# A state-space layer gated by a feed-forward layer: two generator sums in one burst, and two shared PSUM banks

## The chip, the cores and the metric

The kernel runs on one core of a Trainium2 chip. The metric is the device time of one execution in microseconds (us), from the first to the last instruction and the little around them. All times below come from timed runs or from one execution that the hardware profiler recorded.

## What is computed

The input `u` has 2048 positions of 512 channels. It is normalised, and then goes two ways whose results are multiplied:

```python
xn = layernorm(u)                               # over the 512 channels
# s: a convolution of each channel with a kernel K of 2048 taps
dt = exp(log_dt);  P[d,n,l] = exp(dt[d] * (A_re + 1j*A_im)[d,n] * l)
K  = einsum("dn,dnl,dn->dl", C, P, dt * B).real # 512 channels, 128 modes each
s  = irfft(rfft(xn, 4096) * rfft(K, 4096))[:2048] + xn * Dskip
# g: a feed-forward layer of width 1792
g  = silu(gelu(xn @ w1 + b1) @ w2 + b2)
out = u + s * g
```

## The kernel before

**Front and back.** The program has a front (the list `ORDER`, up to `gk.close()`) and a back (the convolution by discrete Fourier transforms in matmuls, functions `first_dft` to `rows_out`). In the front two pieces of work are interleaved by hand.

The first is the feed-forward layer. It goes over four blocks of 512 positions and 14 blocks of 128 hidden units, in two passes of 7 hidden blocks; a step j is one pair (positions, hidden block), 56 in all. Each operand is split into a high and a low part, so that each product needs three matmuls of 512 columns. For a step, `F.j.0` and `F.j.1` are the first layer on TensorE (`first_half`, lines 256 to 258, into one of two PSUM banks named f1), `G.j` the gelu on ScalarE (line 270), `H.j` the rounding to the high part on ScalarE (line 276), `R.j` the low part on VectorE (line 282), and `S.j.0` to `S.j.3` the second layer on TensorE (`second_part`, lines 295 to 297, into four PSUM banks named z). `W`, `WB` and `WS` load and split weights: `WS.f.0` and `.1` round the two weight blocks (w1h, w2h) on ScalarE, `.2` and `.3` take the rest (w1l, w2l) on VectorE.

The second is the generator, which makes the convolution kernel K for 16 channels at a time, 32 groups s in all. For each half h of a group, `A.s.h` makes phases by one bf16 matmul (line 595), `B.s.h` rounds them (ScalarE or VectorE), `C.s.h` takes the rest (VectorE, line 609) and so frees the bank. `N.s` takes the sines on ScalarE, `Z.s` the magnitudes on GpSimd, `E.s.0` to `.2` multiply both into tables e on VectorE (lines 641 to 648; two buffers of tables). `Q.s` sums over the 128 modes in 64 small matmul passes (line 656), `U.s` copies the sums out of PSUM on ScalarE (line 662) and `UD.s` stores them by a DMA of the sync engine's queue (SP).

**What sets the order.** Each engine works off its own queue in order. `ORDER` is a list of such pieces: the program emits each piece's instructions in the order of the list, so the list sets every queue's order. Weight DMAs, stores of the sums and reloads all go through SP's queue. Tile waits are inserted by the framework: an instruction waits for the producers of its inputs and for the last readers of the buffer that it writes.

**PSUM.** f1 has two banks and z has four; phases have one bank (tag ph) and the sums have one (tag sm). The small turns `T`, `pT` and `sm_turn` borrow one of these two.

**Back.** After the list, two last steps of the second layer run between the first transforms; then come the tables `mc` (line 798) and the transforms (line 883 on), which need all stored sums of a block of 128 channels (`kernel_load`, line 848).

Of the kernel before, what the change touches and what calls it, by code (L numbers as in the profile page):

```python
# [11 lines left out]
F32 = mybir.dt.float32  # L12
# [8 lines left out]
P = 128  # L21
L, D, NS, F = 2048, 512, 128, 1792
G = D // P
# [25 lines left out]
WS.0.3 LD.0 LD.1 WS.1.0 WS.1.1 P.0 P.0 W.2 G.0 H.0 WB.2 P.0 WS.1.2 P.0 F.1.0 P.0 LS.3.1 LS.2.0 R.0 S.0.0  # L49
W.3 WS.2.0 LS.3.0 WS.2.1 LL.4 WS.1.3 LL.5 S.0.1 LS.2.1 WS.2.2 F.1.1 WB.3 F.2.0 WS.2.3 WS.3.0 S.0.2 F.2.1  # L50
G.1 W.4 P.0 H.1 WB.4 WS.4.0 WS.4.1 P.1 WS.3.1 S.0.3 WS.3.2 F.3.0 P.0 F.3.1 W.5 P.0 R.1 P.0 G.2 P.0
WS.3.3.1 WS.4.2 LS.5.0 WB.5 G.3 H.2 S.1.0 LS.4.0 F.4.0 P.0 F.4.1 H.3 P.0 LR.2 S.1.1 S.1.2 R.2 LC.2 KL.0.0
G.4 S.1.3 W.6 S.2.0 WS.4.3.1 S.2.1 R.3 A.0.0 H.4 KL.1.0 LC.3 TF.2.0 S.2.2 S.2.3 TH.2.0 B.0.0 WS.5.0
TF.3.0 WS.5.1 C.0.0 TH.3.0 WB.6 BB TL.2.0 A.0.1 WS.5.2 KL.0.1 Z.0 S.3.0 TL.3.0 B.0.1 TF.3.1 TH.3.1 C.0.1
TL.3.1 WS.5.3.1 P.1 LD.2 P.0 LD.3 WS.6.0 S.3.1 WS.6.1 S.3.2 S.3.3 A.1.0 LS.5.1 TF.2.1 N.0.0 TH.2.1 F.5.0
LS.4.1 B.1.0.1 F.5.1 KL.1.1 WS.6.2 TL.2.1 N.0.1 G.5 C.1.0 R.4 F.6.0 LK.0 S.4.0 S.4.1 A.1.1 KL.2.0 F.6.1
B.1.1 LR.4 E.0.0 H.5 F.7.0 G.6 Z.1 F.7.1 WS.6.3 C.1.1 H.6 A.2.0 F.8.0 S.4.2 E.0.1 E.0.2 KL.2.1 R.5 N.1.0
N.1.1 B.2.0.1 Q.0 R.6 G.7 Z.2 LC.4 C.2.0 E.1.0 E.1.1 KL.3.0 F.8.1 S.4.3 U.0 H.7 S.5.0 G.8 S.5.1 A.2.1
B.2.1 KL.3.1 P.1 LD.4 F.9.0 C.2.1 TF.4.0 KL.4.0 UD.0 R.7 LC.5 F.9.1 E.1.2 S.5.2 P.1 N.2.0 G.9 TH.4.0
S.5.3 A.3.0 TF.4.1 LL.6 S.6.0 Q.1 S.6.1 H.8 B.3.0.1 C.3.0 S.6.2 S.6.3 TL.4.0 A.3.1 KL.4.1 N.2.1 O.0.0 U.1  # L60
# [24 lines left out]
WS.7.2 S.24.0 WS.7.3 OK.2 KL.14.1 WS.8.1 H.25 WS.8.2.1 G.26 H.26 WS.9.0 F.27.1 S.24.1 B.14.0 WS.9.1 Z.14
C.14.0 A.14.1 S.24.2 R.25 B.14.1.1 N.13.0 F.28.0 U.10 S.24.3 WS.8.3 C.14.1 G.27 N.13.1 N.14.0 Q.11 U.11
# [1088 lines left out]
```

## Time and profile before

| | |
|---|---|
| three timed runs | 560.06, 561.87 and 561.93 us, median 561.87 us |
| profiled execution, first to last instruction | 558.0 us (the page gives no other time for it) |
| the front ends, by the first matmul of the transforms | 391.8 us |
| matmuls recorded on TensorE | 7179 |
| copies of sums, stores of sums | 32 and 32 |

The median stands 3.9 us above the profiled span, for what lies around it and for the spread of the runs. In the rows below, a number in front is the start in us from the span's start, then the duration; `[x <-Y]` is the time that the engine stood idle before it and who ended that. Line numbers are those of the kernel before. PE is TensorE's matmul side and PEld its weight loads, DVE is VectorE, ACT is ScalarE, POOL is GpSimd, SPq is the sync engine's DMA queue. The end of a matmul is modelled, so the distance from start to start says more than the duration.

### The profile page before, as it was taken

What the parts mean: (1) busy time and instruction counts of PE and PEld (TensorE: products, weight loads), DVE (VectorE), ACT (ScalarE), POOL (GpSimd) and SP (SyncE); (2) the same over time, 40 slices, a digit from 0 to 9 for tenths busy, and PEclk for the clock granted to TensorE, in tenths of its full rate; (3) what the DMA queues carried; (4) which work ended last, traced back from release to release, by engine and by line L of the source; (5) the groups of instructions that cost most, each with busy time, mean ns of one, the idle gap of its engine ahead of it and who ended that gap; (6) DMA issues with size and microseconds to landing.
All of it is one profiled execution on the core that took longest, in us unless ns stands there. A gap on an engine that the chain in (4) does not pass through costs nothing.

```text
span 558.0 us, 17143 instructions
## 1 busy us (share of the span) xinstructions
PE 540.2 (97%) x7179; PEld 432.1 (77%) x7179; DVE 454.2 (81%) x697; ACT 407.8 (73%) x602; POOL 296.3 (53%) x403
## 2 busy tenths in 40 slices
PE   8899999999999999999999999999999999999995
PEld 7567777777777777767777777777889998988872
DVE  6899999999997799988988969877357657767874
ACT  3589997977598999668989798995355565564542
POOL 5639585776966769857718747540320305014323
PEclk9999999999999999999999999999999999999999
DMA  8959337267468392426167049205965583615945
GB/s 188 288 161 311 84 96 210 61 210 228 135 189 269 133 295 81 143 75 192 57 188 219 21 114 186 61 11 181 365 245 79 140 128 95 191 46 127 197 120 113
DMA packets 108345, 86.92 MB, mean 156 GB/s; under 512 B 44294, under 2 KB 87562, under 8 KB 108268
## 3 DMA queue, kind: packets, MB, share of 16 engines
q1 hardware_dynamic: 97584, 65.37, 43.8%
q0 software_dynamic: 9568, 19.93, 12.1%
q8 instruction: 56, 0.92, 0.7%
q10 hardware_dynamic: 1116, 0.53, 0.4%
q14 instruction: 21, 0.17, 0.1%
HBM read 52.25 MB, written 33.55 MB: 154 GB/s over the span
## 4 chain that ended last, share of the span: by engine, by line
PE 68%; DVE 16%; issue 6%; DMA 5%; SPq 2%; ACT 1%; POOL 1%; DVEq 0%; POOLq 0%
PE z L295 8%; PE z L296 7%; PE z L297 7%; PE f L256 7%; PE f L258 7%; PE f L257 7%; PE s L883 6%; PE kg L656 5%; PE s L864 4%; PE sa L918 3%; DMA w2s<-in_B_w_dram 2%; PE ph L595 2%; PE w L936 2%; DVE e L641 2%; DVE hl L282 2%
## 5 line engine op out<-in xcount | busy, mean ns | idle before, releaser
L618 POOL TENSOR_TENSOR mm<-mm,rc 128x32 f32<-128x32 f32 (+4 forms) x150 | 110.7, 738 | 11.8
L295 PE MATMUL z<-w2h,hh 128*128 128x512 f32 x224 | 97.9, 437 | 0.0
L256 PE MATMUL f<-xh,w1h 128*128 128x512 f32 x220 | 92.0, 418 | 0.5 <-ACT hf L270 0.5
L297 PE MATMUL z<-w2h,hl 128*128 128x512 f32 x224 | 88.5, 395 | 0.9 <-DVE hl L282 0.9
L296 PE MATMUL z<-w2l,hh 128*128 128x512 f32 x224 | 88.7, 396 | 0.0
L258 PE MATMUL f<-xh,w1l 128*128 128x512 f32 x220 | 86.9, 395 | 1.5 <-DVE w1l L241 1.5
L257 PE MATMUL f<-xl,w1h 128*128 128x512 f32 x220 | 86.7, 394 | 0.0
L883 PE MATMUL s<-X,mc 64*64 64x128 f32 x2048 | 63.5, 272 | 0.9 <-issue 0.9
L900 DVE TENSOR_TENSOR t<-s,uh 128x512 f32<-128x512 f32 x64 | 41.1, 685 | 25.9 <-ACT uh L891 25.6
L883 PEld LDWEIGHTS s<-X,mc 64*64 64x64 f32 x2048 | 56.0, 133 | 4.8 <-issue 2.7
L641 DVE TENSOR_TENSOR e<-mm,ra 128x1024 f32<-128x1024 f32 x32 | 47.8, 1495 | 4.7 <-POOL mm L618 3.2
L297 PEld LDWEIGHTS z<-w2h,hl 128*128 128x128 f32 x224 | 42.1, 188 | 11.7 <-DVE hl L282 1.8
L258 PEld LDWEIGHTS f<-xh,w1l 128*128 128x128 f32 x220 | 41.3, 188 | 11.9 <-DVE w1l L241 2.1
L615 POOL COPY mm<-rc 128x32 f32<-128x32 f32 x30 | 15.4, 512 | 65.4 <-DVE e L648 49.0
L256 PEld LDWEIGHTS f<-xh,w1h 128*128 128x128 f32 x220 | 41.5, 189 | 10.3 <-ACT hf L270 1.2
L282 DVE TENSOR_TENSOR hl<-hf,hh 128x512 fp32r<-128x512 f32 x56 | 46.7, 838 | 3.4 <-ACT hh L276 3.3
L295 PEld LDWEIGHTS z<-w2h,hh 128*128 128x128 f32 x224 | 42.5, 190 | 9.0
L609 DVE SCALAR_TENSOR_TENSOR ra<-ra,ph 128x512 f32<-128x512 f32 x64 | 43.6, 681 | 6.9 <-ACT ra L603 6.0
L296 PEld LDWEIGHTS z<-w2l,hh 128*128 128x128 f32 x224 | 42.3, 189 | 7.9
L257 PEld LDWEIGHTS f<-xl,w1h 128*128 128x128 f32 x220 | 41.4, 188 | 8.9
L870 ACT COPY X<-s 128x512 f32<-128x512 f32 x56 | 28.9, 598 | 25.6 <-PE s L864 25.6
L645 DVE TENSOR_TENSOR e<-mm,ra 128x1024 f32<-128x1024 f32 x32 | 45.6, 1425 | 0.0
(185 smaller groups left out, 1146.2 us busy)
## 6 DMA issues: line engine op xcount, KB each, us to landing
x<-in_A_u_dram SPq DMA_DIRECT2D x16, 256.0 KB
xs<-x SPq DMA_DIRECT2D x16, 256.0 KB
xt_h<-xh POOLq DMA_DIRECT2D x4, 1024.0 KB, 5.4
xt_l<-xl POOLq DMA_DIRECT2D x4, 1024.0 KB, 7.3
kgd<-ko SPq DMA_DIRECT2D x32, 128.0 KB
za<-zo SPq DMA_DIRECT2D x4, 1024.0 KB
xh<-xt_h POOLq DMA_DIRECT2D x4, 1024.0 KB, 6.8
xl<-xt_l POOLq DMA_DIRECT2D x4, 1024.0 KB, 10.1
```

The costliest lines, as they stand in the source:

```text
L256: PE.matmul(p, wh[:, k, :], xh[:, k, :], start=(k == 0), stop=False)
L257: PE.matmul(p, wh[:, k, :], xl[:, k, :], start=False, stop=False)
L258: PE.matmul(p, wl[:, k, :], xh[:, k, :], start=False, stop=(k == KD - 1))
L282: V.tensor_sub(hl, hf, hh)
L295: PE.matmul(z, hh[:, s], wh, start=(f0 == 0 and not rows), stop=False)
L296: PE.matmul(z, hh[:, s], wl, start=False, stop=False)
L297: PE.matmul(z, hl[:, s], wh, start=False, stop=(f0 == FA - 1))
L609: V.scalar_tensor_tensor(ra[:, 0, c], ra[:, 1, c], MAGIC, p, op0=ALU.subtract, op1=ALU.subtract)
L618: GP.tensor_mul(mv[:, :, 0:3:2, w:2 * w], mv[:, :, 0:3:2, 0:w], rc[:, 2 + 2 * i:4 + 2 * i, :].rearrange("p j c -> p c j").unsqueeze(3).to_ ...
L641: V.tensor_mul(e1, m1.unsqueeze(1).to_broadcast([P, 2, CH, N1]), ra[:, :, :, :N1])
L645: V.tensor_mul(e2[:, :, :, :H], m2[:, :, :H].unsqueeze(1).to_broadcast([P, 2, CH, H]), ra[:, :, :, dn])
L883: PE.matmul(p[ka * 64:(ka + 1) * 64, r, o, :, jj], mc[h, k, ((0, 2), (1, 0))[c][o], :], xf[b][h, c, :, k, :], start=(c == 0), stop=(c == 1 ...
```

## The change

`Q`, `U` and `UD` now take a pair of groups: `Q.j` sums the groups 2j and 2j+1 in one burst of 128 matmul passes into one full bank of 512 columns; one copy and one store follow. Phases, sums and the small turns share two banks under one tag with two buffers, in turn. The list `ORDER` is another one throughout, and some lookups keep a key for each half or block, since two may be open at once.

```diff
-WS.0.3 LD.0 LD.1 WS.1.0 WS.1.1 P.0 P.0 W.2 G.0 H.0 WB.2 P.0 WS.1.2 P.0 F.1.0 P.0 LS.3.1 LS.2.0 R.0 S.0.0
+P.0 WS.1.0 WS.1.1 WS.0.3 W.2 WS.1.2 WB.2 P.0 W.3 F.1.0 P.0 G.0 F.1.1 H.0 G.1 R.0 H.1 WS.2.0 LS.3.1 S.0.0
...
     def gen_phase(s, h):
-        p = pss.tile([P, HC, NPH], F32, tag="ph", name=f"ph{s}_{h}")
+        p = pss.tile([P, HC, NPH], F32, tag="ph", name=f"ph{s}_{h}", bufs=2)
...
-        gen[s]["ph"] = p
+        gen[s]["ph", h] = p
...
-    def gen_sum(s):
-        e1, e2 = gen[s]["e"]
-        p = pss.tile([P, DD, N2], F32, tag="sm", name=f"kg{s}")
-        for d in range(DD):
-            for c in range(2):
-                for g in range(G):
-                    PE.matmul(p[g * N1:(g + 1) * N1, d, :], e1[:, c, g * DD + d, :], e2[:, c, g * DD + d, :],
-                              start=(c == 0), stop=(c == 1), skip_group_check=True)
-        gen[s]["p"] = p
+    def gen_sum(j):
+        p = pss.tile([P, 2, DD, N2], F32, tag="ph", name=f"kg{j}", bufs=2)
+        for i in range(2):
+            e1, e2 = gen[2 * j + i]["e"]
+            for d in range(DD):
+                for c in range(2):
+                    for g in range(G):
+                        PE.matmul(p[g * N1:(g + 1) * N1, i, d, :], e1[:, c, g * DD + d, :], e2[:, c, g * DD + d, :],
+                                  start=(c == 0), stop=(c == 1), skip_group_check=True)
+        gen[2 * j]["p"] = p
...
-        gen[s]["ko"] = ko = par.tile([P, DD, N2], F32, tag="ko", name=f"ko{s}", bufs=2)
-        A.copy(ko, gen[s]["p"])
+        gen[2 * j]["ko"] = ko = par.tile([P, 2, DD, N2], F32, tag="ko", name=f"ko{j}")
+        A.copy(ko, gen[2 * j]["p"])
...
-        SY.dma_start(kgd[b][:, j * DD * N2:(j + 1) * DD * N2], gen.pop(s)["ko"].rearrange("p a b -> p (a b)"))
+        SY.dma_start(kgd[b][:, i * w:(i + 1) * w], gen.pop(2 * j)["ko"].rearrange("p i a b -> p (i a b)"))
```

Counted over the whole program, the copies of sums fall from 32 to 16, the stores of sums from 32 to 16, and the loads of a ScalarE function table from 61 to 58; the counts of all other instructions on all engines stay the same.

How the queues move is seen at three places. The first is VectorE's queue at the start, from the low part of hidden block 0's second weight (`w2l0`) on; `pr0` are parameters of the generator, `w1l1` is the low part of block 1's first weight, for which the step F.1 waits, and `hl_0_0` is the low part for S.0. Before:

```order
L241 TENSOR_TENSOR w2l0_255<-w2s0_139,w2h0_254 128x512
L508 TENSOR_TENSOR pr0_ci_351<-pr0_bi_339,pr0_cr_340 128x128
L509 TENSOR_TENSOR pr0_br_352<-pr0_bi_339,pr0_cr_340 128x128
L510 TENSOR_TENSOR pr0_m_353<-pr0_cr_340,pr0_bi_339 128x128
L512 TENSOR_SCALAR pr0_bi_357<-pr0_ci_351 128x128
L513 RECIPROCAL pr0_bi_357<-pr0_bi_357 128x128
L514 TENSOR_TENSOR pr0_bi_357<-pr0_bi_357,pr0_br_352 128x128
L241 TENSOR_TENSOR w1l1_324<-w1s1_214,w1h1_323 128x512
```

Now:

```order
L235 TENSOR_TENSOR w2l0_255<-w2s0_139,w2h0_254 128x512
L235 TENSOR_TENSOR w1l1_329<-w1s1_214,w1h1_328 128x512
L502 TENSOR_TENSOR pr0_ci_353<-pr0_bi_340,pr0_cr_341 128x128
L503 TENSOR_TENSOR pr0_br_354<-pr0_bi_340,pr0_cr_341 128x128
L504 TENSOR_TENSOR pr0_m_355<-pr0_cr_341,pr0_bi_340 128x128
L506 TENSOR_SCALAR pr0_bi_359<-pr0_ci_353 128x128
L507 RECIPROCAL pr0_bi_359<-pr0_bi_359 128x128
L508 TENSOR_TENSOR pr0_bi_359<-pr0_bi_359,pr0_br_354 128x128
L276 TENSOR_TENSOR hl_0_0_375<-hf_0_0_363,hh_0_0_371 128x512
```

The low part of block 1's weight has moved ahead of the six parameter instructions.

The second place is ScalarE's queue a little later, from the parameters' arctan on: `hf_0_1` and `hf_0_2` are the gelu of steps 1 and 2, `w1h4`, `w2h4` and `w2h3` roundings of weights just loaded. Before:

```order
L517 ACT_TABLE_LOAD
L517 ACTIVATE pr0_cr_362<-pr0_bi_357 128x128
L239 CAST w1h2_406<-w1s2_343 128x512
L239 CAST w2h2_408<-w2s2_349 128x512
L239 CAST w1h3_445<-w1s3_404 128x512
L270 ACT_TABLE_LOAD
L270 ACTIVATE hf_0_1_460<-f1_0_1_364,b1s_97 128x512
L276 CAST hh_0_1_471<-hf_0_1_460 128x512
L239 CAST w1h4_475<-w1s4_462 128x512
L239 CAST w2h4_477<-w2s4_473 128x512
L239 CAST w2h3_447<-w2s3_435 128x512
L270 ACTIVATE hf_0_2_530<-f1_0_2_437,b1s_97 128x512
```

Now:

```order
L264 ACTIVATE hf_0_1_373<-f1_0_1_346,b1s_97 128x512
L270 CAST hh_0_1_377<-hf_0_1_373 128x512
L233 CAST w1h2_379<-w1s2_335 128x512
L233 CAST w2h2_381<-w2s2_338 128x512
L233 CAST w1h3_399<-w1s3_344 128x512
L511 ACT_TABLE_LOAD
L511 ACTIVATE pr0_cr_420<-pr0_bi_359 128x128
L233 CAST w1h4_429<-w1s4_413 128x512
L233 CAST w2h4_431<-w2s4_416 128x512
L233 CAST w2h3_401<-w2s3_418 128x512
L264 ACT_TABLE_LOAD
L264 ACTIVATE hf_0_2_509<-f1_0_2_437,b1s_97 128x512
```

Step 1's gelu has moved ahead of the arctan and of three weights; step 2's gelu stands behind the same three weights as before, now with a table load ahead of it.

The third place is TensorE's queue at the last sums (`kg`, written from the tables `e` of groups 30 and 31). Before:

```order
L297 MATMUL z_1_4627<-w2h_2712,hl_10_4787 128x512
L656 MATMUL kg_4882<-e_30_4835,e_30_4834 32x64 x32
L295 MATMUL z_2_4628<-w2h_2712,hh_10_4783 128x512
L296 MATMUL z_2_4628<-w2l_2713,hh_10_4783 128x512
L297 MATMUL z_2_4628<-w2h_2712,hl_10_4787 128x512
L295 MATMUL z_3_4629<-w2h_2712,hh_10_4783 128x512
L296 MATMUL z_3_4629<-w2l_2713,hh_10_4783 128x512
L297 MATMUL z_3_4629<-w2h_2712,hl_10_4787 128x512
L656 MATMUL kg_4939<-e_31_4919,e_31_4918 32x64 x32
L295 MATMUL z_0_4626<-w2h_2774,hh_11_4825 128x512
```

Now:

```order
L252 MATMUL f_7_13_4773<-xh_3751,w1l_2911 128x512
L651 MATMUL kg_4840<-e_30_4802,e_30_4801 32x64 x32
L651 MATMUL kg_4840<-e_31_4833,e_31_4832 32x64 x32
L289 MATMUL z_3_4561<-w2h_2375,hh_10_4688 128x512
L290 MATMUL z_3_4561<-w2l_2376,hh_10_4688 128x512
L291 MATMUL z_3_4561<-w2h_2375,hl_10_4698 128x512
L289 MATMUL z_0_4558<-w2h_2811,hh_11_4703 128x512
```

The two bursts (each instruction of the program is two passes in the trace) stand next to each other in one bank, and five pieces S of the second layer, S.52.3 and S.53.0 to S.53.3, follow them. All 16 pairs stand like this in the new queue. The tables of a pair take both table buffers, so the first `E` of the next pair comes behind the burst.

More of the change, by code (lines that the diff above doesn't have):

```diff
@@ L128 @@
+R.55 S.53.0 S.53.1 S.53.2 H.54 S.53.3 R.54
 """
@@ L462, in timestep @@
         yield
-        p = pss.tile([P, G], F32, tag="sm", name="sm_turn")
+        p = pss.tile([P, G], F32, tag="ph", name="sm_turn", bufs=2)
         PE.transpose(p, rows, ident[:G, :G])
@@ L583, in gen_load @@
         elif s < 2:
-            gen[s]["rc"] = SB["rec"][:, s]
+            gen[s]["rc"] = SB["rec", 0][:, s]
         else:
@@ L706, in prologue @@
             ln_scale(n, *moments(n))
-        for q, tag in enumerate(("ph", "sm", "z", "z")):
+        for q, tag in enumerate(("ph", "ph", "z", "z")):
             ln_turn(q // 2, q % 2, tag)
```

166 lines of the change are left out of this document (80 added, 86 removed).

## The prediction

> **What bounds the kernel now.** I begin with the page: span, busy times, and the chain of work that ended last.
>
> ```profile
> span 558.0 us, 17143 instructions
> PE 540.2 (97%) x7179; PEld 432.1 (77%) x7179; DVE 454.2 (81%) x697; ACT 407.8 (73%) x602; POOL 296.3 (53%) x403
> PE 68%; DVE 16%; issue 6%; DMA 5%; SPq 2%; ACT 1%; POOL 1%; DVEq 0%; POOLq 0%
> ```
>
> TensorE is busy for 97% and holds 68% of the chain. The stages (view of windows: length, then busy us and count of PE, PEld, DVE, ACT, POOL) say where it has company:
>
> ```profile
> 0.00:35.00 35.00, 28.71 (x146) 22.94 (x146) 27.28 (x74) 17.08 (x30) 16.77 (x49) 1.00 0.87 220
> 35.00:140.00 105.00, 104.22 (x885) 80.92 (x886) 100.03 (x178) 92.58 (x142) 75.18 (x101) 1.00 0.58 172
> 140.00:391.50 251.50, 250.40 (x2547) 191.87 (x2546) 217.18 (x282) 212.32 (x277) 159.78 (x205) 1.00 0.50 141
> 391.50:558.00 166.50, 156.93 (x3603) 136.38 (x3601) 109.70 (x165) 85.79 (x155) 44.55 (x50) 0.99 0.61 154
> ```
>
> From 35 to 391.5 us TensorE is idle for 0.78 + 1.10 = 1.9 us in all. So in the front a microsecond of TensorE's own work is a microsecond of the end, and only the first 35 us have large gaps. VectorE is second: 100.0 of 105 us early, 217 of 251.5 later. The granted clock is 1.00 in the front and stays so. The back (166.5 us) is not changed and follows the front's last matmuls; I move it as a block.
>
> **Term 1: one burst for two sums.** TensorE's timeline around the last but one burst, and the group's row (busy us, then mean ns of one):
>
> ```profile
> 383.69 0.40 PE L295 MATMUL z<-w2h,hh 128*128 128x512 f32 x1
> 383.93 0.40 PE L296 MATMUL z<-w2l,hh 128*128 128x512 f32 x1
> 384.16 0.40 PE L297 MATMUL z<-w2h,hl 128*128 128x512 f32 x1
> 384.48 1.10 PE L656 MATMUL kg<-e,e 128*32 128x64 f32 x64
> 385.51 0.50 PE L295 MATMUL z<-w2h,hh 128*128 128x512 f32 x1
> 385.85 0.40 PE L296 MATMUL z<-w2l,hh 128*128 128x512 f32 x1
> 386.09 0.40 PE L297 MATMUL z<-w2h,hl 128*128 128x512 f32 x1
> L656 PE MATMUL kg<-e,e 128*32 128x64 f32 x2048 | 35.2, 221 | 0.0
> ```
>
> A 512-column matmul starts every 0.235 us. From the start at 384.16 to that at 385.85 pass 1.69 us, of which two such steps are 0.47: a burst costs 1.22 us. Inside it the 64 starts span 1.10 - 0.22 = 0.88 us, 14 ns apart; the other 0.34 us are its entry and exit (0.32 and 0.34 us where a step takes 0.235, and the last sums draining). A pair in one burst pays that once: 1.22 + 64 x 0.014 = 2.12 us in place of 2.44. Sixteen pairs save 16 x 0.32 = **5.1 us**. The bounds are 0 (if each half of a merged burst still pays its own) and 16 x 0.34 = 5.4. I take 5.1, since nothing but the bank's address changes between the halves.
>
> **Term 2: the start.** Idle stretches of TensorE in the first 35 us, VectorE's rows that end the first, and the weight DMAs from the chain:
>
> ```profile
> 20.49 0.50 PE L258 MATMUL f<-xh,w1l 128*128 128x512 f32 x1 [1.51 <-DVE w1l L241]
> 22.70 0.51 PE L297 MATMUL z<-w2h,hl 128*128 128x512 f32 x1 [0.30 <-DVE hl L282]
> 34.02 0.50 PE L297 MATMUL z<-w2h,hl 128*128 128x512 f32 x1 [0.57 <-DVE hl L282]
> 35.04 0.50 PE L256 MATMUL f<-xh,w1h 128*128 128x512 f32 x1 [0.52 <-ACT hf L270]
> 17.58 0.28 DVE L508 TENSOR_TENSOR pr_ci<-pr_bi,pr_cr 128x128 f32<-128x128 f32 x1
> 19.75 0.68 DVE L241 TENSOR_TENSOR w1l<-w1s,w1h 128x512 fp32r<-128x512 f32 x1
> 26.48 6.76 DMA w2s<-in_B_w_dram
> 27.66 1.28 ACT L270 ACT_TABLE_LOAD   x1
> 34.31 1.26 ACT L270 ACTIVATE hf<-f,b1s 128x512 f32<-128x512 f32 x2
> ```
>
> In the new queue w1l of block 1 goes ahead of the six parameter instructions, so it starts at 17.6 and not at 19.75: the first gap, 1.51 us, closes. TensorE then has F.1 (12 matmuls from 18.35), S.0 (14 with the bias rows), F.2 (12), S.1.0, S.1.1, F.3 and S.1.2 (21) before F.4: 59 x 0.235 = 13.9 us, up to 32.2. F.4 needs step 2's gelu to free its bank, and that stands behind the rounding of three weights as today. Their last DMA now waits for the same kind of rest on VectorE, 1.0 to 1.5 us earlier than 26.48, since block 2's loads no longer stand behind the stores of x; but a table load of 1.28 us now stands ahead of the gelu. So gelu 2 ends, and F.4 starts, at about 35.0 as before. The difference is what was done by then: S.1.1 and S.1.2 as well, 6 x 0.235 = **1.4 us**. Bounds: 2.9 us saved (all four gaps gone), and about 0 (the DMAs no earlier, so that 1.28 us of table load stand against the 1.4).
>
> **Term 3: waits for the one phase bank.** Both gaps of TensorE after 35 us end with C (line 609) freeing that bank:
>
> ```profile
> 123.88 0.67 DVE L609 SCALAR_TENSOR_TENSOR ra<-ra,ph 128x512 f32<-128x512 f32 x1
> 124.61 0.66 PE L369 MATMUL xT<-ident,x 128*128 128x128 f32 x4 [0.74 <-DVE ra L609]
> 242.98 0.68 DVE L609 SCALAR_TENSOR_TENSOR ra<-ra,ph 128x512 f32<-128x512 f32 x1
> 243.80 0.38 PE L595 MATMUL ph<-cbs,lh 96*128 96x512 bf16 x1 [1.10 <-DVE ra L609]
> ```
>
> With two banks, the next phase starts while C works. The gaps go, and with each the overlap lost at a restart (a matmul lasts 0.40 and the next starts after 0.235): 0.74 + 1.10 + 2 x 0.165 = **2.2 us**. Bounds: 0 and 2.2.
>
> **Term 4: what the new list adds.** Sums now take a bank that phases want, and a pair fills both table buffers, so VectorE's next E waits for the whole burst and holds back what is queued behind it: the hl of the feed-forward layer, which S needs, and C. Today no E waits for sums:
>
> ```profile
> L641 DVE TENSOR_TENSOR e<-mm,ra 128x1024 f32<-128x1024 f32 x32 | 47.8, 1495 | 4.7 <-POOL mm L618 3.2 <-ACT ra L629 0.7 <-issue 0.4
> ```
>
> The trace does not show this wait. Its bounds for TensorE are 0 and, if each of the 15 hand-overs costs the burst's extra length of 2.12 - 1.22 = 0.9 us, 13.5 us. In the list some pieces of other work stand between most bursts and the next E. I take **3.0 us lost**: near the 2.2 us that the present list leaves in such waits, and some more for the added kind.
>
> **What costs nothing.** ScalarE has 16 copies fewer, and the rest are twice as wide:
>
> ```profile
> L662 ACT COPY ko<-kg 128x256 f32<-128x256 f32 x32 | 11.8, 368 | 4.8 <-PE kg L656 4.8
> L891 ACT COPY uh<-s 128x512 f32<-128x512 f32 x32 | 18.8, 586 | 25.9 <-PE s L883 16.8 <-issue 8.0 <-ACT bs L944 1.0
> ```
>
> A copy of 512 columns takes 586 ns, so 32 x 0.368 - 16 x 0.586 = 2.4 us go, and three table loads of 1.28, 3.8 us; all beside a TensorE that has no gap. SP has 16 issues fewer. At the front's end I checked three things. The last phase, today at 376.0, and the tables made of it:
>
> ```profile
> L595 PE MATMUL ph<-cbs,lh x64: 376/390/393, 41.4 to 376.0; 96*128 96x512 bf16 x64
> 385.00 0.68 DVE L648 SCALAR_TENSOR_TENSOR e<-mm,ra 128x512 f32<-128x512 f32 x1
> 390.95 1.99 SPq L798 DMA_DIRECT2D mc<-in_cm_dram  x4
> 405.89 1.96 PE L883 MATMUL s<-X,mc 64*64 64x128 f32 x58
> ```
>
> That path takes 385.68 - 376.0 = 9.7 us; in the new queue three F halves, five S and one burst stand between last phase and last burst, 3 x 1.41 + 5 x 0.705 + 2.1 = 9.9 us: just covered, and a queueing delay there would show at once. The last store waits for the copy before it, since the new copy has one buffer; it then has the five S behind the burst (3.5 us) as cover. And mc is issued right after the last store, 14.9 us before its first use today; five S instead of four stand behind the burst, so it keeps that cover.
>
> **Sum.** -5.1 - 1.4 - 2.2 + 3.0 = -5.7 us. The profiled span of 558.0 becomes 552.3; the 3.9 us between span and median stay, and the median of 561.87 becomes **556.2 us**. With term 4 at 0 it would be 553.2, at 5.5 us 558.7: the forecast's own range.
>
> **Rivals.** (a) *Given back in the list.* Steps now share tighter turns of the f1 banks (F.13 begins one S, one turn and one phase after the end of F.12, whose bank it takes). If such waits and those of term 4 come to 8 us, the time is 561.87 - 8.7 + 8 = 561.2. Against it: the present list holds its 356 us with 1.9 us idle. Chance 17%. (b) *The hand-over of the tables, slower.* In the stretch to 140 us VectorE has only 5 us free. If each hand-over costs 0.9 us there and later, 13.5 us replace the 3.0: 566.7. It passes today's time when a hand-over costs TensorE more than 8.7 / 15 = 0.58 us. Against it: 34 us free on VectorE after 140. Chance 7%. (c) *The burst runs out of instructions.* The page's row of the queue that brings them:
>
> ```profile
> q8 instruction: 56, 0.92, 0.7%
> ```
>
> 0.92 MB in 56 packets are 16.4 KB each, and by TensorE's 2 x 7179 instructions 64 bytes each: a packet is 256 instructions, as many as a merged burst has (128 loads, 128 matmuls). A packet takes 0.7% of 16 x 558 us / 56 = 1.1 us; a merged burst uses one up in about 1.9. If every burst waited half a packet, 16 x 0.55 = 8.8 us come on top: 565.0. For it: a rate of instructions that no stretch of this trace holds so long; against: the fetch takes less time than the use. The Trainium skill ("Runtime: NRT & Kernel Launch", Instruction fetch mechanics) says that instructions come in blocks of 256, fetched ahead while the block before is worked off, so that crossing a block is mostly hidden; by that rule the sum stays as it is, and the row's size of a packet agrees with it. Chance 4%.
>
> That the change doesn't do what it says is excluded by the order: all pairs stand in one run.
>
> **Chances.** Forecast 72%, (a) 17%, (b) 7%, (c) 4%. The range holds most of the forecast and of (a): 553.0 to 561.5; above it lie (b), (c) and the worst of (a). Half a percent, about what a measurement of this kernel can tell from no change, is 2.8 us. Faster than 559.06: the forecast and a little of (a), 0.74. Slower than 564.68: nearly all of (b) and (c), 0.10. Between: 0.16.
>
> **What would show it.** Term 1: kg rows of 128 with one entry and one exit, about 2.1 us from neighbour to neighbour. Term 2: no gap at F.1, one of 2 to 3 us before F.4 at about 35 us. Term 3: no PE gap that ends with line 603 (609 of before). Term 4: DVE e waiting for PE kg, and PE waiting for hl or for hf. Rival (c): a pause inside kg bursts with no releaser. I am wrong if PE's idle time between 35 us and the front's end is over 6 us, or if the back's 166.5 us change by over 1 us.

## The result, and the profile after

| | before | changed |
|---|---|---|
| median of the timed runs | 561.06 us (560.06 to 561.93) | 577.77 us (575.47 to 582.45) |
| ratio | 1 | 1.0313, 95% interval 1.0262 to 1.0365 |
| profiled execution, first to last instruction | 558.0 us | 573.7 us |
| the front's end (first matmul of the transforms) | 391.8 us | 408.1 us |

The change made the kernel 3.1% slower. Forecast were 556.2 us and a range up to 561.5. The kernel before stands at 561.06 us here, since a fourth run was added to the three. The page after: span, busy times, chain of work that ended last.

```profile
span 573.7 us, 17079 instructions
PE 540.2 (94%) x7179; PEld 434.2 (76%) x7179; DVE 459.0 (80%) x697; ACT 402.3 (70%) x583; POOL 300.4 (52%) x403
PE 46%; DVE 28%; ACT 12%; issue 5%; POOL 4%; DMA 3%; SPq 2%; DVEq 0%; ACTq 0%; POOLq 0%
```

TensorE is as busy as before, 540.2 us, but its part of the chain has fallen from 68% to 46%: VectorE (16% to 28%) and ScalarE (1% to 12%) now set the time over long stretches. The view of windows shows where (length, then busy us and count of PE, PEld, DVE, ACT, POOL, granted clock, DMA share, GB/s).

```profile
0.00:35.00 35.00, 31.00 (x165) 26.27 (x165) 28.25 (x70) 18.20 (x31) 19.68 (x50) 1.00 0.79 198
35.00:140.00 105.00, 100.24 (x802) 77.01 (x801) 97.25 (x171) 85.15 (x128) 66.89 (x94) 0.98 0.63 183
140.00:408.10 268.10, 252.50 (x2618) 194.69 (x2616) 223.46 (x292) 213.29 (x270) 173.10 (x214) 0.99 0.50 136
408.10:573.70 165.60, 156.47 (x3602) 136.27 (x3601) 110.06 (x165) 85.67 (x155) 40.71 (x46) 0.99 0.60 147
```

The start is better (31.0 us of TensorE's work in the first 35 us, 28.7 before) and the back is as before (165.6 us, 166.5 before). All the loss lies between: TensorE idles 4.8 us of 105, then 15.6 of 268, where before left 1.9 us in the whole stretch. It comes gradually. The 60th matmul of the feed-forward layer starts at 29.2 us (31.9 before), the 600th at 185.8 (185.6), the 1000th at 307.4 (297.5), the 1300th at 397.5 (381.8).

Summed by who ended it, TensorE's idle time from 30 us to the front's end is 20.3 us, against 2.9 before: 10.0 us of phases and sums that wait for VectorE's wrap (C, line 603, 609 before), 4.6 us of the second layer that waits for hl (line 276), 2.5 us with no releaser, 1.4 us for a load of phase factors, and small ones. The front's end came 16.3 us later. Of that, 17.4 us are more idle time there; 1.2 us less idle ahead of 30 us (two gaps of 1.8 us in all gone, others longer) and 5.1 us less in bursts go off; some 2.3 us for 14 more restarts at 0.165 us and about 2.9 us at half clock (below) come on top. This adds up.

The burst itself does what was forecast; TensorE's timeline of the changed kernel:

```profile
119.60 0.40 PE L291 MATMUL z<-w2h,hl 128*128 128x512 f32 x1
119.92 1.99 PE L651 MATMUL kg<-e,e 128*32 128x64 f32 x128
121.85 0.50 PE L289 MATMUL z<-w2h,hh 128*128 128x512 f32 x1
122.19 0.40 PE L290 MATMUL z<-w2l,hh 128*128 128x512 f32 x1
```

From 119.60 to 122.19 pass 2.59 us; less two steps of 0.235, that is 2.12 us for 128 passes. Eleven of the 16 bursts cost 2.11 to 2.13 us.

Here are two of the waits, with what stood ahead of them. First at 98 us, rows of GpSimd, VectorE and TensorE:

```profile
90.20 3.84 POOL L612 TENSOR_TENSOR mm<-mm,rc 128x32 f32<-128x32 f32 x5
94.12 1.05 POOL L614 TENSOR_TENSOR mm<-mm,rc 128x512 f32<-128x512 f32 x1
93.07 1.12 DVE L525 SCALAR_TENSOR_TENSOR pr_ci<-pr_ci,sm_dt,pr_br 128x128 f32<-128x128 f32 x1
94.12 1.14 DVE L526 TENSOR_SCALAR pr_ar<-pr_ar,sm_dt 128x128 f32<-128x128 f32 x1
95.18 0.28 DVE L527 TENSOR_SCALAR pr_ai<-pr_ai,sm_dt 128x128 f32<-128x128 f32 x1
...
97.66 1.15 DVE L535 TENSOR_TENSOR pr_cr<-pr_cr,pr_bi 128x128 f32<-128x128 f32 x1
98.97 1.02 DVE L539 SCALAR_TENSOR_TENSOR pr_cr<-pr_m,pr_cr 128x128 f32<-128x128 f32 x1
100.25 0.68 DVE L276 TENSOR_TENSOR hl<-hf,hh 128x512 fp32r<-128x512 f32 x1
95.45 3.21 POOL L612 TENSOR_TENSOR mm<-mm,rc 128x32 f32<-128x32 f32 x5
98.73 1.11 POOL L614 TENSOR_TENSOR mm<-mm,rc 128x512 f32<-128x512 f32 x1
100.99 0.79 PE L291 MATMUL z<-w2h,hl 128*128 128x512 f32 x1 [2.85 <-DVE hl L276]
```

VectorE does parameter pieces of 128 columns. Four of those shown take 1.0 to 1.15 us beside GpSimd's magnitudes (lines 612, 614); where nothing runs on GpSimd the same lines take 0.28 to 0.35. The low part hl stands behind them, and TensorE waits 2.85 us for it. Then the stretch up to 330 us:

```profile
310.43 0.24 POOL L609 COPY mm<-rc 128x32 f32<-128x32 f32 x1 [15.54 <-DMA rc<-recd]
310.75 3.19 POOL L612 TENSOR_TENSOR mm<-mm,rc 128x32 f32<-128x32 f32 x5
313.98 1.23 DVE L635 TENSOR_TENSOR e<-mm,ra 128x1024 f32<-128x1024 f32 x1 [4.59 <-PE z L291]
315.12 2.07 DVE L639 TENSOR_TENSOR e<-mm,ra 128x1024 f32<-128x1024 f32 x1
...
322.59 2.07 DVE L639 TENSOR_TENSOR e<-mm,ra 128x1024 f32<-128x1024 f32 x1
324.58 0.68 DVE L276 TENSOR_TENSOR hl<-hf,hh 128x512 fp32r<-128x512 f32 x1
325.19 0.68 DVE L641 TENSOR_TENSOR e<-mm,ra 128x512 f32<-128x512 f32 x1
325.79 0.70 DVE L642 SCALAR_TENSOR_TENSOR e<-mm,ra 128x512 f32<-128x512 f32 x1
326.41 0.68 DVE L599 TENSOR_SCALAR ra<-ph 128x512 f32<-128x512 f32 x1
327.12 0.69 DVE L603 SCALAR_TENSOR_TENSOR ra<-ra,ph 128x512 f32<-128x512 f32 x1
324.51 0.39 PE L291 MATMUL z<-w2h,hl 128*128 128x512 f32 x1
327.87 0.39 PE L589 MATMUL ph<-cbs,lh 96*128 96x512 bf16 x1 [2.97 <-DVE ra L603]
330.37 3.15 PE L651 MATMUL kg<-e,e 128*32 128x64 f32 x128 [2.11 <-DVE ra L603]
```

From 314 us on VectorE is hardly idle; it is late. Its first table part starts 4.59 us after the piece before it. The profile names a matmul as what ended this wait, but GpSimd's five multiplications end at 313.94, and they started late, since the load of their factors landed only after GpSimd had stood 15.54 us. Then two table parts take 2.07 us each in place of some 1.20. The wraps stand behind all this, and the next phase and then the burst want the banks that wraps free: 2.97 and 2.11 us of TensorE.

### The profile page after: what moved, and what is told of

Its sections match the earlier page's. It is cut to its first block, busy times and chain, and to the rows that moved or that the text cites. A ratio compares the mean times of both kernels' runs of the same rounds, so it can differ in the third digit from the quotient of the medians.

```text
span 573.7 us, 17079 instructions
## 1 busy us (share of the span) xinstructions
PE 540.2 (94%) x7179; PEld 434.2 (76%) x7179; DVE 459.0 (80%) x697; ACT 402.3 (70%) x583; POOL 300.4 (52%) x403
## 4 chain that ended last, share of the span: by engine, by line
PE 46%; DVE 28%; ACT 12%; issue 5%; POOL 4%; DMA 3%; SPq 2%; DVEq 0%; ACTq 0%; POOLq 0%
PE s L879 10%; PE s L860 6%; PE sa L914 5%; DVE e L639 4%; PE z L289 3%; PE z L291 3%; PE z L290 3%; PE f L250 3%; PE f L251 3%; PE f L252 3%; PE w L932 3%; DVE hl L276 2%; DVE e L635 2%; DVE e L642 2%; DVE e L641 2%
## 5 line engine op out<-in xcount | busy, mean ns | idle before, releaser
L612 POOL TENSOR_TENSOR mm<-mm,rc 128x32 f32<-128x32 f32 (+4 forms) x150 | 114.7, 765 | 11.8
L289 PE MATMUL z<-w2h,hh 128*128 128x512 f32 x224 | 95.9, 428 | 0.0
L250 PE MATMUL f<-xh,w1h 128*128 128x512 f32 x220 | 93.4, 425 | 0.4 <-ACT hf L264 0.4
L276 DVE TENSOR_TENSOR hl<-hf,hh 128x512 fp32r<-128x512 f32 x56 | 48.6, 872 | 16.0 <-ACT hh L270 16.0
L609 POOL COPY mm<-rc 128x32 f32<-128x32 f32 x30 | 14.0, 467 | 84.8 <-DVE e L642 41.4
L635 DVE TENSOR_TENSOR e<-mm,ra 128x1024 f32<-128x1024 f32 x32 | 41.9, 1309 | 18.0 <-PE z L291 4.6
L264 ACT ACTIVATE hf<-f,b1s 128x512 f32<-128x512 f32 x56 | 38.3, 688 | 24.5 <-PE f L252 11.7
L639 DVE TENSOR_TENSOR e<-mm,ra 128x1024 f32<-128x1024 f32 x32 | 46.9, 1467 | 0.0
```

The costliest lines, as they stand in the source:

```text
L250: PE.matmul(p, wh[:, k, :], xh[:, k, :], start=(k == 0), stop=False)
L276: V.tensor_sub(hl, hf, hh)
L289: PE.matmul(z, hh[:, s], wh, start=(f0 == 0 and not rows), stop=False)
L612: GP.tensor_mul(mv[:, :, 0:3:2, w:2 * w], mv[:, :, 0:3:2, 0:w], rc[:, 2 + 2 * i:4 + 2 * i, :].rearrange("p j c -> p c j").unsqueeze(3).to_ ...
L635: V.tensor_mul(e1, m1.unsqueeze(1).to_broadcast([P, 2, CH, N1]), ra[:, :, :, :N1])
L639: V.tensor_mul(e2[:, :, :, :H], m2[:, :, :H].unsqueeze(1).to_broadcast([P, 2, CH, H]), ra[:, :, :, dn])
```

## The experiments

Four theories were held against each other. HAND-OVER: a pair of tables fills both buffers, so VectorE waits for the burst. BANKS: phases and sums in turn in two banks wait for each other. LIST: the new order itself, whatever the bursts and banks. CONTENTION: VectorE stretched beside GpSimd. Three came later: LOADS (factors are loaded too late), LATE SIZES (table parts wait for late magnitudes) and SUPPLY (TensorE runs out of instructions). In the table, "idle" is TensorE's idle time from 30 us to the front's end in the profiled execution, and "VectorE" is the sum of the durations of its instructions in the front; neighbours overlap a little, so its busy time there is some 28 us less. Each ratio is taken against runs of the kernel before from the same session, whose medians lie between 560.4 and 560.8 us.

| run | median us | ratio to before, 95% interval | front's end | idle | VectorE |
|---|---|---|---|---|---|
| before | 561.06 | | 391.8 | 2.9 | 372 |
| changed | 577.77 | 1.0313 [1.0262, 1.0365] | 408.1 | 20.3 | 377 |
| pairs_alone | 568.76 | 1.0132 [1.0104, 1.0160] | 399.9 | 11.9 | 364 |
| share_alone | 558.78 | 0.9970 [0.9952, 0.9989] | 391.2 | 2.1 | 375 |
| both_old_list | 562.86 | 1.0043 [1.0022, 1.0064] | 394.0 | 8.6 | 369 |
| new_list_single | 586.23 | 1.0446 [1.0406, 1.0486] | 420.7 | 23.6 | 373 |
| new_list_no_handover | 575.07 | 1.0254 [1.0221, 1.0288] | 407.6 | 18.1 | 373 |
| new_list_early_loads | 570.23 | 1.0168 [1.0138, 1.0198] | 403.0 | 15.5 | 377 |
| new_list_no_sizes | 554.72 | 0.9891 [0.9860, 0.9922] | 387.3 | 4.1 | 340 |
| old_list_tuned | 563.63 | 1.0045 [1.0023, 1.0068] | 395.3 | 9.2 | 369 |
| new_list_no_size_wait | 581.88 | 1.0372 [1.0291, 1.0454] | 412.1 | 22.5 | 381 |
| before_no_sizes | 557.15 | 0.9926 [0.9899, 0.9953] | 389.9 | 1.0 | 339 |
| old_list_no_handover | 558.29 | 0.9951 [0.9934, 0.9968] | 391.4 | 5.1 | 372 |
| pairs_where_free | 558.84 | 0.9966 [0.9941, 0.9990] | 391.0 | 3.2 | 373 |
| new_list_light_sizes | 558.43 | 0.9964 [0.9938, 0.9990] | 389.7 | 5.9 | 342 |
| new_list_split_burst | 582.02 | 1.0365 [1.0338, 1.0391] | 415.4 | 19.3 | 382 |

**The parts of the change, one at a time.**

```diff
 # pairs_alone: old list, pairs in a bank of their own, one bank for phases
-        p = pss.tile([P, 2, DD, N2], F32, tag="ph", name=f"kg{j}", bufs=2)
+        p = pss.tile([P, 2, DD, N2], F32, tag="sm", name=f"kg{j}", bufs=1)
 # share_alone: old list, single sums (set against the kernel before)
-        p = pss.tile([P, DD, N2], F32, tag="sm", name=f"kg{s}")
+        p = pss.tile([P, DD, N2], F32, tag="ph", name=f"kg{s}", bufs=2)
 # both_old_list: the changed kernel with the old list, each Q.j ahead of the
 # first table part that would overwrite its tables
 # new_list_single: the new list, Q.2j and Q.2j+1 in place of Q.j
```

> The old list with one part of the change: two groups are summed in one burst of 128 passes, into a full bank of the sums' own; phases keep their single bank, nothing is shared. Each burst stands ahead of the first table part that would overwrite its tables (in 12 of 16 pairs at or near where the second group's burst was). Theory HAND-OVER (the pair of tables, which fills both buffers, makes VectorE wait for the burst and so delays all else on VectorE): the 5.1 us of the bursts are gained and 8 or more lost, so 564 to 575 us, and VectorE's idle time ahead of the first table part is near 18 us as in the changed kernel. Theory BANKS (phases and sums in turn in two banks make TensorE wait for copies and wraps) and theory LIST (the new order packs tables, phases and sums so that VectorE is late) both expect this kernel to be no slower than before: 555 to 560 us, with the front's end at 386 to 390 us against 391.8.

> The old list and 32 single sums, but phases, sums and small turns share two banks in turn; four copies of sums stand earlier so that their bank is free in time. Theory BANKS: TensorE waits for wraps and copies of two allocations ago, 5 us or more in all, 566 to 572 us. Theories HAND-OVER and LIST: no loss from the sharing, and the two old waits for the single phase bank (0.74 and 1.10 us) go: 558 to 562 us.

> The old list with both parts, pairs in one burst and two shared banks, as in the changed kernel; only the list is the old one (bursts placed as in the run with pairs alone, a few copies earlier). Theory LIST: no slower than before, 554 to 560 us. Theory HAND-OVER: 564 to 575 us. Theory BANKS: 561 to 567 us, with waits of TensorE's phase and sum matmuls for VectorE's wrap of 5 us or more in all.

> The new list with the pairs undone: 32 single sums, the first group's burst moved to a few matmul pieces behind its last table part, the second where the pair's burst was; the two banks are still shared. Theory LIST: the bursts cost their 5.1 us again and the rest stays, 575 to 585 us. Theory HAND-OVER: each table is free earlier, VectorE's idle time ahead of the first table part falls from 18 us to near 5 us, and the time to 560 to 568 us. Theory BANKS: 575 us or more, since the banks are taken in turn by still more tiles.

Sharing alone gained 0.3%: TensorE's waits for wraps fell from 1.84 to 0.33 us, so BANKS falls on the old list. Pairs alone cost 1.3%, as HAND-OVER expected. Both parts together on the old list are 15 us faster than on the new one (562.86 against 577.77): LIST holds for most of the loss. It does not hold for all of it: this run missed the 554 to 560 us that LIST expected and fell into the range of BANKS (561 to 567), with 5.9 us of waits for wraps. The new list with single sums is the slowest of the four, so the pairs aren't what makes it slow. What pairs do cost shows in the run with both parts on the old list; VectorE's group of first table parts (busy us, mean ns, idle us before them and what ended it), then the timeline of both engines around one hand-over:

```profile
L633 DVE TENSOR_TENSOR e<-mm,ra 128x1024 f32<-128x1024 f32 x32 | 45.8, 1431 | 22.8 <-PE kg L649 17.4 <-POOL mm L610 3.5 <-ACT ra L621 1.4
```

```profile
205.34 1.99 PE L649 MATMUL kg<-e,e 128*32 128x64 f32 x128
206.67 1.23 DVE L633 TENSOR_TENSOR e<-mm,ra 128x1024 f32<-128x1024 f32 x1 [3.33 <-PE kg L649]
...
208.41 1.53 DVE L637 TENSOR_TENSOR e<-mm,ra 128x1024 f32<-128x1024 f32 x1
209.87 1.53 DVE L639 TENSOR_TENSOR e<-mm,ra 128x512 f32<-128x512 f32 x1
211.33 1.75 DVE L640 SCALAR_TENSOR_TENSOR e<-mm,ra 128x512 f32<-128x512 f32 x1
...
213.71 0.69 DVE L601 SCALAR_TENSOR_TENSOR ra<-ra,ph 128x512 f32<-128x512 f32 x1
...
214.54 0.38 PE L587 MATMUL ph<-cbs,lh 96*128 96x512 bf16 x1 [3.50 <-DVE ra L601]
```

VectorE stands 3.33 us with a table part that waits for the burst. The next three parts then take 2.3 us over their shortest (1.19, 0.66 and 0.67 us) beside GpSimd, and both together show seven us later as a late wrap. In all VectorE idles 17.4 us for bursts, of which two places reach TensorE (3.50 us here, 1.5 at 306 us, stretched parts again in between). With a bank of their own but one bank for phases (pairs_alone) late wraps hold TensorE longer, 8.3 us in all: two banks for phases soften the hand-over.

**The hand-over taken away**, on both lists. The table parts of groups 2 to 31 are written over their sines, and the bursts sum the first two groups' tables.

```diff
+        if s > 1:
+            gen[s]["e"] = SB["e", s % 2]
+            if n == 0:
+                V.tensor_mul(ra[:, :, :, :N1], m1.unsqueeze(1).to_broadcast([P, 2, CH, N1]), ra[:, :, :, :N1])
...
```

> The changed kernel with its list, pairs and shared banks; the table parts of groups 2 to 31 write over their sines in place instead of into the two table buffers, and every burst sums the tables of groups 0 and 1. So no table part waits for a burst any more, and no burst for a table part; all instructions and their sizes are as in the changed kernel. Theory HAND-OVER: 562 to 570 us against 577.8. Theory LIST (other waits of the new order, not this one): 572 to 578 us, with TensorE's waits for VectorE's wrap and hl still over 8 us in the front.

> The run with both parts on the old list, with the table parts of groups 2 to 31 written over their sines in place and every burst summing the tables of groups 0 and 1, so that no table part waits for a burst. On the new list this edit gained 2.7 us. Theory HAND-OVER as the price of pairs on the old list: the 8.6 us of idle gaps of that run fall to 2 to 3 us, 556 to 558 us against 562.9. If its gaps have another cause: 561 us or more.

On the old list the edit gained 4.6 us (562.86 to 558.29), on the new one 2.7 (577.77 to 575.07), which is within the spread of the changed kernel's own runs (575.5 to 582.5). So the hand-over is real on the old list, near the size that the prediction gave it, but it isn't the loss of the changed kernel.

**The sync engine's queue.** Only its order changes:

```diff
 # KL.s.0 (phase factors) mostly 8 entries behind A.(s-2).1 or later,
 # KL.s.1 (magnitude factors) 20 to 88 ahead of Z.s, mostly 44 to 47, where it
 # stood 4 to 88 ahead; stores UD.j mostly at least 22 behind U.j
```

> The changed kernel with only the sync engine's queue in another order: the load of a group's phase factors is issued no earlier than the buffer's last reader allows (8 list entries behind it) and some 35 entries ahead of its use, the load of its magnitude factors some 45 entries ahead of its use where it stood 4 to 66, and the stores of sums at least 22 entries behind their copy. No other engine's order changes. Theory LOADS (the new list has these loads so late, or behind an entry that waits, that GpSimd's magnitudes and with them the table parts come late: GpSimd waited 28.8 us for magnitude factors against 9.6 before): the stalls of 284 to 333 us go, 10 us with the half clock that follows: 565 to 570 us. Theories HAND-OVER and CONTENTION: 575 to 579 us, since nothing that VectorE does changes.

7.5 us came back, just short of what LOADS expected; HAND-OVER and CONTENTION, which expected no gain here, both missed. TensorE's waits at 311, 325 and 328 us shrank to 0.7 us in all, and with them the half clock at 329 us; those at 98 and 229 us stayed (3.15 and 2.35 us).

**GpSimd's magnitudes.** They are left out for groups 2 to 31, on both lists:

```diff
+        if s > 1:
+            gen[s]["mm"] = SB["mm", s % 2]
+            return
```

> The changed kernel, with GpSimd's magnitudes computed for groups 0 and 1 only; later groups reuse those two tiles, so their GpSimd work and its waits are left out (some 7.7 us of GpSimd a group). Theory CONTENTION (VectorE's parts run at up to twice their time beside GpSimd's magnitudes): VectorE's parts of 1.5 to 2.1 us fall to 0.7 to 1.2 us everywhere, and the time to 562 to 568 us. Theory LOADS: 565 to 570 us too, but with the waits at 97 us (VectorE's parameter pieces up to 1.1 us each) still there in part. If neither, 574 us or more.

> The kernel before, with GpSimd's magnitudes computed for groups 0 and 1 only and reused after; the control for the same edit on the changed kernel, which gained 23 us. TensorE's idle gaps in the front of before are 2.9 us in all, so if the old list hides GpSimd's work (theory LIST), it gains 1 to 3 us: 557 to 560 us. If GpSimd's work costs before as much as it costs the changed kernel: 545 us or less.

The edit gained 23.1 us on the new list, more than either theory expected, and 3.7 on the old one. Without GpSimd's work the new list is the faster of the two, 554.7 against 557.2. Its span of 552.4 us is by chance the 552.3 that the prediction summed up to: with this work left out on both lists, the change gained 2.4 us and not 5.7. Three ways were open: VectorE's wait for late magnitudes, GpSimd's queue, or the stretching. The first was tried by leaving the magnitudes in place and letting no table part wait for them:

```diff
-        mm = par.tile([P, CH, N2 + N1], F32, tag="mm", name=f"mm{s}", bufs=2)
+        mm = SB["mm"] if s > 1 else par.tile([P, CH, N2 + N1], F32, tag="mm", name=f"mm{s}", bufs=2)
...
+        gen[s]["mm"] = SB["mm", 0]
```

> The changed kernel with GpSimd's magnitudes computed for every group, at their places and with their loads, but the table parts of all groups read the magnitudes of group 0 (GpSimd's tiles of groups 1 to 31 all go into one other buffer that nothing reads). GpSimd's work beside VectorE stays; only VectorE's wait for it is left out. Theory CONTENTION (VectorE's instructions stretched beside GpSimd): 570 us or more, since all stretching stays. Theory LATE SIZES (the table parts wait for magnitudes that come late, with hl and wraps behind them on VectorE): 556 to 563 us, near the 554.7 us of the run without magnitudes.

No gain (581.88, two runs 6.6 us apart): LATE SIZES falls as the main cause. This profile has 9.5 us of pauses without a releaser, 7.0 more than the changed kernel, and TensorE's waits for wraps and hl fell from 14.6 to 9.6 us, so some 5 us of gain may be hidden in it; that goes with the 7.5 us of earlier loads. Then GpSimd's traffic was taken away and much of its time kept:

```diff
+            for i in range(18):
+                GP.tensor_copy(mm[:, 0, i:i + 1], rc[:, 0, 0:1])
```

> The changed kernel, where for groups 2 to 31 GpSimd does, in the place of the magnitudes, 18 copies of one column each into the same tile: about as long on GpSimd (18 times 0.3 us against some 5.6 us undisturbed), with the same loads, waits and order, but hardly any data moved; the magnitudes of those groups are left out. Theory CONTENTION (GpSimd's traffic stretches VectorE): VectorE's instructions keep their undisturbed times as in the run without magnitudes, 554 to 562 us. Theory GPSIMD'S QUEUE (its time, its loads, and who waits for it): 570 us or more, as with the full magnitudes.

19.3 us came back, though GpSimd is still busy 203 us of the front (260 in the changed kernel, 91 without magnitudes) and waits for the same loads. The copies take 3.9 us of GpSimd a group where the magnitudes take 5.6, so its time was not kept in full. A line of this run's page and groups of it:

```profile
PE 537.2 (97%) x7179; PEld 433.9 (78%) x7179; DVE 424.1 (76%) x697; ACT 401.5 (72%) x583; POOL 243.2 (44%) x733
L610 POOL COPY mm<-rc 128x1 f32<-128x1 f32 x540 | 116.0, 274 | 103.4 <-DVE e L644 42.6
L640 DVE TENSOR_TENSOR e<-mm,ra 128x1024 f32<-128x1024 f32 x32 | 39.4, 1232 | 20.5 <-ACT ra L628 16.6 <-PE kg L656 3.7
L644 DVE TENSOR_TENSOR e<-mm,ra 128x1024 f32<-128x1024 f32 x32 | 39.6, 1237 | 1.0 <-POOL mm L610 1.0
```

VectorE is busy 34.9 us less than in the changed kernel (459.0) with the same 697 instructions: the table parts of 1024 columns are back at a mean of 1.23 us. So CONTENTION is shown: most of what costs the new list its time is VectorE stretched while GpSimd works on data. GpSimd's queue is not the cause, as far as the two runs together tell: taking away the wait for it gained nothing, and keeping three quarters of its busy time kept little of the loss. The traces show the stretching piece by piece too. In the changed kernel all 16 hl and 37 table parts that took over 1.2 times their shortest ran beside a GpSimd instruction; those with nothing on GpSimd beside them stayed within 5% of the shortest. The Trainium skill ("SBUF — State Buffer", Who interferes with whom) says that a VectorE instruction with two inputs in SBUF contends with a GpSimd instruction that reads SBUF, and one with at most one such input, outside VectorE's two-port modes, doesn't. The trace agrees: the wrap, with one input in PSUM, took 654 to 691 ns in all its 64 runs of the changed kernel, 37 of them beside the magnitudes for over half of their time, while hl and the table parts, with two in SBUF, reached 2.5 and 2.1 us. Line 526 does not fit so plainly: with one tensor and a value per partition it took 1.14 us above and 0.28 elsewhere. No run here separates instructions by their inputs alone.

**Is there more stretching in the changed kernel?** No. In the kernel before 22 of 56 hl and 43 of 128 table parts took over 1.2 times their shortest, in the changed one 16 and 37; all VectorE instructions of the front exceed the shortest of their kind by 51.8 us before, 55.2 after. The lists differ in how much of it they bear. For the hl that are first read after 60 us, from the end of an hl to the first matmul that reads it pass 5.96 us in the median before (lower quarter 4.15), 3.71 (2.20) in the changed kernel; without magnitudes 7.58 and 3.93. The new list leaves about half to two thirds of the lead, with or without GpSimd's work. That this lead is why it bears less is argued from these numbers; no run changed it alone. The run with both parts on the old list stands between, with 4.73 (3.12), and lost only 2.2 us against the kernel before.

**Pauses inside bursts.** These are TensorE's rows of one burst in the changed kernel, then in the run without size waits, then in the run with split bursts:

```profile
283.98 1.99 PE L651 MATMUL kg<-e,e 128*32 128x64 f32 x127 [0.84 <-DVE ra L603]
287.59 0.22 PE L651 MATMUL kg<-e,e 128*32 128x64 f32 x1 [1.62 <-issue]
```

```profile
287.79 1.99 PE L654 MATMUL kg<-e,e 128*32 128x64 f32 x127 [1.17 <-DVE ra L603]
294.07 0.22 PE L654 MATMUL kg<-e,e 128*32 128x64 f32 x1 [4.29 <-issue]
```

```profile
291.85 1.09 PE L653 MATMUL kg<-e,e 128*32 128x64 f32 x60
293.64 0.31 PE L653 MATMUL kg<-e,e 128*32 128x64 f32 x4 [0.71 <-issue]
```

```diff
-    def gen_sum(j):
+    def gen_sum(j, i):
 # Q.j.0, then one piece F or S, then Q.j.1
```

> The changed kernel, with each burst of 128 passes in two halves of 64 with one piece of the feed-forward layer (3 or 6 matmuls) between them; same bank, one copy, one store. Theory SUPPLY (a burst of 128 passes and 128 weight loads uses up instructions faster than they arrive in blocks of 256): the pauses inside bursts go (2.0 us in the profile of the changed kernel, 0.4 and 1.6), against 16 more entries of a burst at 0.32 us, 5.1 us; net 2 to 5 us slower, 578 to 583 us, and no pause without a semaphore at those two places. If the pauses stay, or the time falls by more than 2 us, their cause is another.

Split bursts cost 4.2 us (577.77 to 582.02, little more than the two kernels' spread), near the 5.1 of 16 more entries, and the pause at 79 us went while the other shrank from 1.62 to 0.71. In all seven profiles of the new list with pairs, a pause comes after 4771 of TensorE's recorded instructions (4773 once). The places go with the instruction queue's packets of 16 KB, which hold 256 instructions by the prediction's count: in the run without size waits TensorE paused after 948, 3497 and 4771 of its recorded instructions (weight loads and matmuls), when 2, 12 and 17 packets had landed, which is 436, 425 and 419 more than 256 for each packet. The excess is nearly the same each time, and each pause ended 1.2 to 1.5 us after the next packet had landed. This suggests that TensorE had used up all that had arrived; no run changed the supply alone. A burst of 256 instructions in 1.8 us can do that; single bursts of 128 did not in the kernel before, and once, for 0.26 us, in the run with sharing alone.

**Versions to beat both.**

```diff
 # old_list_tuned: both_old_list with Q.6, Q.8, Q.10 earlier, E.14 and E.20.0 later
 # pairs_where_free: share_alone with pairs 0, 1, 3, 12 to 15 in one burst
```

> The run with both parts on the old list, with the two places mended where the pair's tables made VectorE wait for the burst and TensorE then waited for a wrap (3.5 us at 214.5, 1.5 us at 306.3): the bursts of pairs 6, 8 and 10 stand a few matmul pieces earlier, and the table parts of group 14 and the first of group 20 behind the wraps and low parts that TensorE waits for. Theory LIST with HAND-OVER as its price: those 5 us go, the gain of the bursts shows: 556 to 559 us, under both kernels. If the waits only move on: 561 to 564 us.

> The old list and two shared banks, with pairs summed in one burst only where the old list had no table part of the next pair ahead of the second burst (pairs 0, 1, 3 and 12 to 15); the other nine pairs keep two bursts of 64. Seven merges at 0.32 us each are 2.2 us below the 558.8 us of the run with sharing alone: 556 to 558 us if the hand-over costs nothing where the burst has room; 559 to 562 us if it costs there too, or if the one buffer for copied sums holds up ScalarE.

The tuned list missed: the gap of 3.5 us fell to 0.9 and that of 1.5 went, and others of the same sum came (1.85 us for a wrap at 227 us, 2.0 for a copy of sums, 1.2 for a copy of z). Pairs only where they fit are no faster than sharing alone (558.84 and 558.78), though seven merges should save 2.2 us. Both beat the kernel before by 0.3%, and the changed kernel by 3.3%.

## Why the prediction was wrong

**Term 1** (one burst for two sums, -5.1) was right: 2.12 us a pair measured.

**Term 2** (the start, -1.4) was right in sign, but one step of it was wrong: step 2's gelu was to end, and F.4 to start, at about 35.0 us as before, since the loads would come only 1.0 to 1.5 us earlier. The last load landed in time for a rounding at 28.9 us, the gelu started at 30.9 (34.3 before), and F.4 ran from 32.0 without a gap. So the 60th matmul came 2.7 us earlier, near the bound of 2.9.

**Term 3** (waits for the phase bank, -2.2) was right for the sharing alone, which gained 1.9 us on the old list. In the changed kernel the waits for wraps rose to 10.0 us: the second bank did not help where wraps came late.

**Term 4** is the step that failed. It asked what the new list adds, took "3.0 us lost: near the 2.2 us that the present list leaves in such waits", and bounded it by 15 hand-overs. The hand-over did cost some 2.7 us on the new list and 4.6 on the old. But the size of the other waits was taken from the old list, as if a list of the same pieces had the same slack. With the other terms as forecast, the span's 15.7 us of loss make this term 24.4 us. In its place the runs showed that GpSimd's magnitudes, which stretch VectorE, cost the new list 19 to 23 us and the old 3.7; part of the same loss, 7.5 us, came back by earlier loads alone, so these figures don't add up. The free time of VectorE (5 us to 140 us, 34 after) was set against rival (b) as cover, though in the changed kernel much of it lies in waits (4.59 us in one, above) and not ahead of hl and wraps. The trace of before had the warning: a table part's mean of 1495 ns beside a shortest of 1210. Outside the sum, the granted clock was to stay at 1.00 in the front; it was half for 3.4 us twice.

**Rival (a)** named a loss in the list, but by the f1 banks: TensorE waited 0.4 us for hf after 35 us, so that mechanism was not it. **Rival (b)** was priced at 13.5 us and came at 2.7. **Rival (c)** happened, in two bursts of 16 and with 2.0 us, not in all with 8.8. What the Trainium skill ("Runtime: NRT & Kernel Launch", Instruction fetch mechanics) says there, that crossing a block is mostly hidden, holds for the other 14. The sign to be wrong, more than 6 us of TensorE's idle time from 35 us on, was met threefold. How far VectorE's instructions stretch beside GpSimd, and whether the new list has room for it, was not weighed.

## What to carry to other kernels

A new order of the same pieces is not free because every engine has idle time left: measure how long ahead of its use each product is ready, and compare it with how far its producer's instructions stretch beside another engine. When a list is worked out from the durations of instructions alone, try it with the neighbour's traffic taken out, on the old list too: the difference is what the plan doesn't know. Taking parts of a change one by one found a gain (the shared banks) inside a loss.

## What the runs showed of the hardware

**TensorE's clock halves after short idle times.** The windows of the changed kernel around the waits shown above; the first figure behind the five busy times is the granted clock:

```profile
97.00:101.00 4.00, 1.15 (x39) 0.63 (x27) 3.93 (x8) 3.02 (x3) 3.61 (x5) 0.97 0.30 68
101.00:104.00 3.00, 3.00 (x7) 2.20 (x8) 2.90 (x7) 1.84 (x3) 2.17 (x3) 0.50 1.07 335
329.40:332.80 3.40, 2.44 (x93) 2.47 (x97) 3.37 (x7) 3.37 (x5) 3.08 (x6) 0.51 0.16 39
```

Over all 16 profiles, from 25 us to the front's end, there are 19 stretches at half clock, of 3.4 us each (6.8 once). Each began within 1.2 us of the end of a TensorE idle stretch of 1.96 us or more. Of 24 idle stretches of 2.0 us or more, 18 had one so close, and of ten from 1.5 to 2.0 us, one had. One of 3.5 us had none. So a wait of 3 us can cost up to 1.7 us more, by an estimate from these stretches (half of 3.4). The Trainium skill ("TensorE: Matmul & The Clock Gate", What's actually happening) has the half clock after one idle window of about 3.4 us, with windows that run freely beside the work. The runs agree with the length of the slow stretch, and show it after idle times from 1.96 us on.

**VectorE's instructions stretch up to four times** beside GpSimd in the changed kernel: from 0.28 to 1.15 us for 128 columns, from 0.67 to 1.6 us for hl beside the magnitudes, and to 2.5 beside a GpSimd copy (line 835) at the front's end.

**TensorE pauses inside dense bursts**, for 0.4 to 4.3 us where 256 instructions take 1.8 us, at places that the count of landed instruction packets gives.
